# Scale guards on VectorE, and one product for two scales, in a fused attention and two-layer MoE kernel

## The chip, the cores and the metric

The kernel runs on one core of one Trainium2 chip. The metric is the device time of one execution in microseconds, the median of the runs; lower is better.

## The reference

An attention layer feeds two dense layers, over 12288 tokens of 128 channels:

```python
kv_flat = kv_pool.reshape(B, -1, C) @ w_sr        # 768 keys; k = v = kv_flat
s = scale * (q @ k.transpose(0, 2, 1))
a = np.exp(s - s.max(-1, keepdims=True))
x = (a / (a.sum(-1, keepdims=True) + 1e-09)) @ v
...
h = x @ w_in                                       # 128 -> 2048
x = (np.maximum(h, 0.0) + alpha * np.minimum(h, 0.0)) @ w_out
...
h = x @ w_in2
out = (h * (1.0 / (1.0 + np.exp(-1.702 * h)))) @ w_out2
```

## The kernel before, in words

The tokens are cut into 24 blocks of 512 (j = 0 to 23). Tokens lie along the free axis, channels along the 128 partitions. Every float32 operand is split into a float16 part (hi) and a float16 remainder (lo), and every product is three matmuls of 128x512 in PSUM (hi·hi, hi·lo, lo·hi). The TensorE steps of a block are:

- S j,t: the scores of 128 queries against 768 keys, four per block (six matmuls of 384 columns each)
- V j,k: the attention result X, six per block, one for each 128 keys
- L1 j,m and L2 j,m: the first dense layer by 16 slices m of the 2048 hidden channels; L2 sums into the result Y
- L3 j,m and L4 j,m: the second dense layer, likewise; L4 sums into the output

The steps of several blocks are mixed: while block 13's V and X are made, L1 and L2 of block 12 and L3 and L4 of blocks 10 and 11 run. A block's share is 210 matmuls of 512 columns and 24 of 384.

Around each L1 slice ScalarE takes relu from PSUM and VectorE the rest (prelu, L798); around each L3 slice ScalarE takes tanh (L837) and VectorE the rest of the gelu (L839). Then ScalarE rounds to float16 (hi, L774), and GpSimd, or for a few slices VectorE, subtracts for the remainder (lo, L777). L2 and L4 read these. In the text gelu 11,6 is the gelu of block 11's slice 6, and so on.

To split q, X and Y, each needs a power of two as its scale. Three times per block (Q, X and Y) this chain runs:

- a top: VectorE's absolute maximum of each partition (`td`, 128x1 in bfloat16, L613)
- a total: two matmuls of one column with a 128x128 matrix of ones (`total`, L623 for the tops and L624 for the constant `least`, which keeps the sum off zero). It takes one of the three PSUM banks (hb, hb, bk) that L1 and L3 use as well (`pool_h`)
- on VectorE, the exponent (`scp`, a bitwise and, L409), the scale (`scc`, L411), and for q also `qu`, for Y also `yu` (128x2)
- the hi part on ScalarE (L637) and the lo part on VectorE (L639)

For Y, ScalarE first copies the result to SBUF (`yc`, L818).

The order of instructions is fixed before the run. The first some 900 follow a list written out by hand (`ORDER`), and the rest a planner that places them by costs and due times. Each engine takes its instructions in that order, one by one, so an instruction that waits holds up all that follow it on its engine. q is loaded by the queue of SP, which also issues the transposes of the attention weights (`eh`, `el`) and the weights' loads.

Of the kernel before, what the change touches and what calls it, by code (L numbers as in the profile page):

```python
# [28 lines left out]
TB = 512  # L29
# [41 lines left out]
class Op:  # L71
# [41 lines left out]

# [271 lines left out]
def record(nc, T):  # L385
# [71 lines left out]
    def load(fn, size, w, prio, r=(), gate=None, name="load", eng="SP", late=1, occ=470):  # L457
        return op(eng, occ, int(size / 0.41e3), lambda: fn(S if eng == "SP" else A), r, w, prio, gate, name, dma=late)
# [7 lines left out]
    def load_wsr(e):  # L466
        e.dma_start(out=T["wsr"], in_=T["in_wsr"])
        A.preload_act_table(AF.Exp)
    load(load_wsr, 65536, [B["wsr"]], -999, eng="ACT", late=3700, occ=1900)
    load(lambda e: e.dma_start(out=T["al"], in_=T["in_al"]), 8192, [B["al"]], -997, r=[(B["wsr"], None, 7000)], eng="ACT", late=9000)  # L470
# [137 lines left out]

    qh, ql, qsc = {}, {}, {}

# [5 lines left out]

    def total(pool, cols_, least, prio):

        pm = pool.buf("pt")

        def f():
            for i, (c, _) in enumerate(cols_):
                mm(out=pm.ap[:, 0:1], lhsT=T["ones"], rhs=c(), start=i == 0, stop=False)  # L623
            mm(out=pm.ap[:, 0:1], lhsT=T["ones"], rhs=least, start=False, stop=True)  # L624
        op("PE", 28 + 28 * len(cols_), 0, f, [b for _, b in cols_] + [B["ones"]], [pm], prio, name="scmm")
        return pm

    def scale_of(d, pool, kc, kcb, prio):
        pm = total(pool, [(lambda: d.ap, d)], T["least"], prio)
        p, c = new("scp"), new("scc")  # L630
        small(lambda: ts(p.ap, pm.ap[:, 0:1].bitcast(I32), 0x7F800000, ALU.bitwise_and), [pm], [p], prio, occ=117)
        small(lambda: ts(c.ap, p.ap, -1.0, ALU.mult, kc(), ALU.add), [p] + kcb, [c], prio + .01, occ=110, dur=200)
        return c, p

    def parts(j, hi, lo, x, xb, c, prio, gate=None, psum=True):
# [4 lines left out]
                                                           op0=ALU.mult, op1=ALU.subtract), [xb, c, hi], [lo], prio + .01, gate, name="lo", lock=not psum)  # L640

    def q_prep(j, prio, gate=None, pool=None):
        t = q_t[j]
        pl.tag = f"Q{j}"
        d = top_of(j, lambda: cols(t.ap, j), t, False, prio, gate)
        c, p = scale_of(d, pool or pool_x, lambda: float(268 << 23), [], prio + .1)
        qh[j], ql[j] = new("qh"), new("ql")
        parts(j, qh[j], ql[j], lambda: cols(t.ap, j), t, c, prio + .2, gate, psum=False)
        qsc[j] = p
        if j:  # L650
            q_scale(j, prio + .3)
        pl.tag = ""

    def q_scale(j, prio):
        u, p = new("qu"), qsc[j]
        small(lambda: ts(u.ap, p.ap.bitcast(F32), T["kq"], ALU.mult), [p, B["kq"]], [u], prio, occ=125, dur=205)
        qsc[j] = u
# [81 lines left out]
    def x_prep(j, prio):  # L739
        x = xacc[j]  # L740
        pl.tag = f"X{j}"
        d = top_of(j, lambda: cols(x.ap, j), x, True, prio, None)
        c, p = scale_of(d, pool_h, lambda: T["kxc"], [B["kxc"]], prio + .1)
        xh[j], xl[j] = new("xh"), new("xl")
        parts(j, xh[j], xl[j], lambda: cols(x.ap, j), x, c, prio + .2)
        xsc[j] = p
        pl.tag = ""
# [64 lines left out]
    def y_prep(j):  # L812
# [6 lines left out]
        d = top_of(j, lambda: cols(y.ap, j), y, True, pr, None)  # L819
        c, p = scale_of(d, pool_h, lambda: T["kyc"], [B["kyc"]], pr + .5)  # L820
        u = new("yu")
        xp = xsc[j]
        small(lambda: ts(u.ap, T["kk"], p.ap.bitcast(F32), ALU.mult, xp.ap.bitcast(F32), ALU.mult), [B["kk"], p, xp], [u], pr + .6,
              occ=190, dur=280, lock=True)
# [81 lines left out]
    def rest():  # L906
# [3 lines left out]
        for j in range(NB):  # L910
            for m in range(KF):
                s = KF * j + m
                for jj in range(2, NB):
                    a = KF * jj - 25 + (ATT_AT[jj - 2] if jj < 4 else 0)
                    gate = lambda x: steps[s]
                    if s == max(a - 7, 0):
                        load_q(jj, s, steps.get(s - 1))
# [43 lines left out]

RINGS = {"q": 2, "fold": 2, "kv": 12, "raw": 6, "cv": 2, "td": 4, "scp": 16, "scc": 6, "qh": 2, "ql": 2, "qu": 4, "nm": 4,
         "sm": 4, "r": 4, "e": 2, "ah": 2, "alo": 2, "eh": 2, "el": 2, "xh": 2, "xl": 2, "yh": 3, "yl": 3, "yc": 1, "yu": 6,
# [4 lines left out]
def attn_moe_kernel(ctx: ExitStack, tc: tile.TileContext, q, kv, w_sr, w_in1, w_out1, alpha, w_in2, w_out2, out):  # L968
# [29 lines left out]
    for key in ("w1", "w2", "w3", "w4"):  # L998
        T["wm_" + key] = t("wm" + key, [NCW], BF16)
        T["wt_" + key] = t("wt" + key, [1], F32)  # L1000
        for x in ("we", "g", "u", "b"):
            T[x + "_" + key] = t(x + key, [1], I32)

    shapes = {"q": ([TB], F32), "raw": ([CW, 2], I32), "cv": ([CW], I32), "fold": ([KV2 // 2], F32), "td": ([1], BF16),
              "scp": ([1], I32), "scc": ([1], I32), "qh": ([TB], F16), "ql": ([TB], F16), "qu": ([1], F32), "nm": ([1], F32),
# [76 lines left out]
```

## Time and profile before

| | |
|---|---|
| time, median of 3 runs | 1244.88 us (1244.63 to 1245.29) |
| the profiled execution's own time | 1247.91 us |
| its span | 1246.1 us |
| TensorE busy | 1217.7 us, 98% |
| VectorE busy | 977.2 us, 78% |
| ScalarE busy | 1104.3 us, 89% |
| GpSimd busy | 799.1 us, 64% |
| mean granted TensorE clock | 0.998 |

The span is what the trace covers; the profiled execution's own time is 1.8 us longer, and it lies 3.0 us above the median of the runs without a profile. The busy shares are means over the start, where weights and keys are prepared, 18 blocks that repeat almost exactly, and a tail.

### The profile page before, as it was taken

What the parts mean: (1) busy time and instruction counts of PE and PEld (TensorE: products, weight loads), DVE (VectorE), ACT (ScalarE), POOL (GpSimd) and SP (SyncE); (2) the same over time, 40 slices, a digit from 0 to 9 for tenths busy, and PEclk for the clock granted to TensorE, in tenths of its full rate; (3) what the DMA queues carried; (4) which work ended last, traced back from release to release, by engine and by line L of the source; (5) the groups of instructions that cost most, each with busy time, mean ns of one, the idle gap of its engine ahead of it and who ended that gap; (6) DMA issues with size and microseconds to landing.
All of it is one profiled execution on the core that took longest, in us unless ns stands there. A gap on an engine that the chain in (4) does not pass through costs nothing.

```text
span 1246.1 us, 18536 instructions
## 1 busy us (share of the span) xinstructions
PE 1217.7 (98%) x5919; PEld 574.5 (46%) x5922; DVE 977.2 (78%) x1796; ACT 1104.3 (89%) x1939; POOL 799.1 (64%) x688
## 2 busy tenths in 40 slices
PE   6699999999999999999999999999999999999998
PEld 4444444444444444444444444444444444444443
DVE  5999997877777877777778777777787877776766
ACT  1799888989999999899999998999999989988988
POOL 1567556676667566666675666666766766666764
PEclk9999999999999999999999999999999999999999
DMA  9922222121222121212211222212121222120000
GB/s 378 219 51 46 40 56 47 35 55 26 56 49 33 43 47 35 55 31 51 55 27 43 47 42 49 40 41 56 27 49 41 47 43 48 34 47 14 9 9 18
DMA packets 165378, 66.69 MB, mean 54 GB/s; under 512 B 156448, under 2 KB 156576, under 8 KB 164256
## 3 DMA queue, kind: packets, MB, share of 16 engines
q1 hardware_dynamic: 164992, 65.43, 23.1%
q8 instruction: 46, 0.75, 0.3%
q14 instruction: 52, 0.43, 0.1%
q10 hardware_dynamic: 288, 0.07, 0.0%
HBM read 21.05 MB, written 6.29 MB: 22 GB/s over the span
## 4 chain that ended last, share of the span: by engine, by line
PE 64%; ACT 0%; issue 0%; DVE 0%; POOL 0%; POOLq 0%; ACTq 0%
PE bk L444 14%; PE bk L446 14%; PE bk L445 14%; PE hb L444 6%; PE hb L445 6%; PE hb L446 6%; PE sa L672 1%; PE sa L673 1%; PE sa L676 1%; POOL arena L777 0%; ACT arena L774 0%; ACT arena L837 0%; POOLq L1078 0%; ACT arena L796 0%; DVE arena L798 0%
## 5 line engine op out<-in xcount | busy, mean ns | idle before, releaser
L777 POOL TENSOR_TENSOR arena<-arena 128x512 f16<-128x512 f32 x656 | 763.0, 1182 | 401.9 <-ACT arena L774 205.1
L774 ACT CAST arena<-arena 128x512 f16<-128x512 f32 x740 | 443.6, 624 | 52.1 <-PE bk L445 19.4
L798 DVE SCALAR_TENSOR_TENSOR arena<-arena,oma,hb 128x512 f32<-128x512 f32 x280 | 207.7, 742 | 57.5 <-ACT arena L796 54.6
L839 DVE SCALAR_TENSOR_TENSOR arena<-arena,hb 128x512 f32<-128x512 f32 x225 | 153.7, 683 | 43.1 <-ACT arena L837 39.6
L796 ACT ACTIVATE arena<-hb 128x512 f32<-128x512 f32 x280 | 167.1, 597 | 8.7 <-POOL arena L777 4.7
L837 ACT ACTIVATE arena<-hb,yu 128x512 f32<-128x512 f32 x225 | 156.7, 696 | 13.0 <-PE hb L446 6.1
L446 PE MATMUL bk<-arena,w4h 128*128 128x512 f16 x384 | 145.5, 379 | 0.2 <-POOL arena L777 0.2
L446 PE MATMUL bk<-arena,w2h 128*128 128x512 f16 x384 | 145.5, 379 | 0.2 <-POOL arena L777 0.2
L444 PE MATMUL bk<-arena,w2h 128*128 128x512 f16 x384 | 145.5, 379 | 0.1
L445 PE MATMUL bk<-arena,w4l 128*128 128x512 f16 x384 | 145.5, 379 | 0.0
L445 PE MATMUL bk<-arena,w2l 128*128 128x512 f16 x384 | 145.5, 379 | 0.0
L444 PE MATMUL bk<-arena,w4h 128*128 128x512 f16 x384 | 145.5, 379 | 0.0
L711 DVE SCALAR_TENSOR_TENSOR alo<-sa,r,ah 128x768 f16<-128x768 f32 x88 | 89.4, 1016 | 53.7 <-ACT ah L696 52.4
L839 DVE SCALAR_TENSOR_TENSOR arena<-arena,bk 128x512 f32<-128x512 f32 x159 | 108.4, 682 | 23.3 <-ACT arena L837 23.1
L837 ACT ACTIVATE arena<-bk,yu 128x512 f32<-128x512 f32 x159 | 109.4, 688 | 17.6 <-PE bk L446 16.7
L444 PE MATMUL hb<-xh,w1h 128*128 128x512 f16 x280 | 106.3, 380 | 1.8 <-ACT xh L637 0.9
L446 PE MATMUL hb<-xl,w1h 128*128 128x512 f16 x280 | 106.3, 380 | 0.2 <-DVE xl L639 0.2
L445 PE MATMUL hb<-xh,w1l 128*128 128x512 f16 x280 | 106.3, 380 | 0.0
L682 DVE TENSOR_REDUCE nm<-sa 128x1 f32<-128x768 f32 x94 | 89.5, 952 | 12.4 <-PE hb L624 7.2
L777 DVE TENSOR_TENSOR arena<-arena 128x512 f16<-128x512 f32 x112 | 87.1, 778 | 6.3 <-ACT arena L774 4.7
L798 DVE SCALAR_TENSOR_TENSOR arena<-arena,oma,bk 128x512 f32<-128x512 f32 x104 | 77.3, 743 | 16.6 <-ACT arena L796 14.6
L689 ACT ACTIVATE sa<-sa,nm,qu 128x768 f32<-128x768 f32 x88 | 85.0, 966 | 1.2 <-DVE nm L409 1.1
(151 smaller groups left out, 2105.7 us busy)
## 6 DMA issues: line engine op xcount, KB each, us to landing
q<-in_q SPq DMA_DIRECT2D x24, 256.0 KB, 3.0
arena<-in_kv SPq DMA_DIRECT2D x12, 512.0 KB, 8.9
out<-arena SPq DMA_DIRECT2D x24, 256.0 KB, 2.0
raw<-in_moe_w_in SPq DMA_DIRECT2D x4, 1024.0 KB, 13.8
raw<-in_moe_w_out SPq DMA_DIRECT2D x4, 1024.0 KB, 12.1
eh<-ah SPq DMA_TRANSPOSE x96, 2.7
el<-alo SPq DMA_TRANSPOSE x96, 2.8
wsr<-in_w_sr ACTq DMA_DIRECT2D x1, 64.0 KB, 3.3
```

The costliest lines, as they stand in the source:

```text
L444: mm(out=o, lhsT=wh, rhs=xh, start=start, stop=False)
L445: mm(out=o, lhsT=wl, rhs=xh, start=False, stop=False)
L446: mm(out=o, lhsT=wh, rhs=xl, start=False, stop=stop)
L682: op("DVE", 868, 956, lambda: V.tensor_reduce(out=nm.ap, in_=s.ap[:, :, 0:HALF], axis=AX.XY, op=ALU.max, negate=True), [s], [nm], prio + . ...
L689: op("ACT", 890, 985, lambda: A.activation(dst(), src(), AF.Exp, bias=nm.ap, scale=qsc[j].ap, accum_out=sm.ap), [s, nm, qsc[j]], [e, sm], ...
L711: op("DVE", 933, 1019, lambda: V.scalar_tensor_tensor(out=al.ap, in0=dst(), scalar=r.ap, in1=ah.ap, op0=ALU.mult, op1=ALU.subtract), [e, r ...
L774: op("ACT", act(508, n), act(618, n), lambda: A.copy(cols(hi.ap, j), cols(g.ap, j)), [g], [hi], s + 1.2, name=f"{nm}h{j},{m}")
L777: lambda: (V if on else G).tensor_tensor(out=cols(lo.ap, j), in0=cols(g.ap, j), in1=cols(hi.ap, j), op=ALU.subtract),
L796: op("ACT", act(488, n), act(597, n), lambda: A.activation(cols(g.ap, j), cols(h.ap, j), AF.Relu, scale=-1.0), [h], [g], s + .3, name=f"re ...
L798: op("DVE", dve(658, n), dve(746, n), lambda: V.scalar_tensor_tensor(out=cols(g.ap, j), in0=cols(g.ap, j), scalar=T["oma"][:, m:m + 1], in ...
L837: op("ACT", act(581, n), act(687, n), lambda: A.activation(cols(g.ap, j), cols(h.ap, j), AF.Tanh, scale=u.ap[:, 0:1]), [h, u], [g], s + .3 ...
L839: op("DVE", dve(605, n), dve(687, n), lambda: V.scalar_tensor_tensor(out=cols(g.ap, j), in0=cols(g.ap, j), scalar=1.0, in1=cols(h.ap, j), ...
```

## The change

- The constant `least` and its matmul go from the totals of blocks 3 and up (`j > 2`), in Q, X and Y. In its place VectorE takes the maximum of the tops and 2^-60, in SBUF and in place, ahead of the total (called the guard here).
- In blocks 3 to 21, the top of the queries of block j + 2 is taken beside that of X of block j, into the two columns of a new tile `td2` (128x2, bfloat16). One guard of 128x2 and one matmul with two columns serve both, then one bitwise and of 128x2 (`scp2`), and the scales `scc` for X and `qcc` for the queries. The queries' own totals of blocks 5 to 23 go.
- From block 5 on a block's queries are loaded six steps m earlier.
- The planner's cost of a total goes from 28 + 28 ns for each of its matmuls to 62 ns for each, and that of loading `w_sr` changes; `ORDER` is renumbered and 19 entries shorter.

```diff
-    def total(pool, cols_, least, prio):
+    def total(pool, cols_, least, prio, n=1):
 
         pm = pool.buf("pt")
 
         def f():
             for i, (c, _) in enumerate(cols_):
-                mm(out=pm.ap[:, 0:1], lhsT=T["ones"], rhs=c(), start=i == 0, stop=False)
-            mm(out=pm.ap[:, 0:1], lhsT=T["ones"], rhs=least, start=False, stop=True)
-        op("PE", 28 + 28 * len(cols_), 0, f, [b for _, b in cols_] + [B["ones"]], [pm], prio, name="scmm")
+                mm(out=pm.ap[:, 0:n], lhsT=T["ones"], rhs=c(), start=i == 0, stop=least is None and i == len(cols_) - 1)
+            if least is not None:
+                mm(out=pm.ap[:, 0:n], lhsT=T["ones"], rhs=least, start=False, stop=True)
+        op("PE", 62 * len(cols_) + (62 if least is not None else 0), 0, f, [b for _, b in cols_] + [B["ones"]], [pm], prio, name="scmm")
         return pm
 
-    def scale_of(d, pool, kc, kcb, prio):
-        pm = total(pool, [(lambda: d.ap, d)], T["least"], prio)
+    def scale_of(d, pool, kc, kcb, prio, j=0):
+        if j > 2:
+            small(lambda: ts(d.ap, d.ap, 2.0 ** -60, ALU.max), [d], [d], prio)
+        pm = total(pool, [(lambda: d.ap, d)], None if j > 2 else T["least"], prio)
...
     def q_prep(j, prio, gate=None, pool=None):
         t = q_t[j]
         pl.tag = f"Q{j}"
-        d = top_of(j, lambda: cols(t.ap, j), t, False, prio, gate)
-        c, p = scale_of(d, pool or pool_x, lambda: float(268 << 23), [], prio + .1)
+        if j in qc:
+            c, p = qc[j]
+        else:
+            d = top_of(j, lambda: cols(t.ap, j), t, False, prio, gate)
+            c, p = scale_of(d, pool or pool_x, lambda: QC, [], prio + .1, j)
...
     def x_prep(j, prio):
         x = xacc[j]
         pl.tag = f"X{j}"
-        d = top_of(j, lambda: cols(x.ap, j), x, True, prio, None)
-        c, p = scale_of(d, pool_h, lambda: T["kxc"], [B["kxc"]], prio + .1)
+        if 2 < j < NB - 2:
+            t, d, p2, c, qc_ = q_t[j + 2], new("td2"), new("scp2"), new("scc"), new("qcc")
+            op("DVE", dve(593, TB), dve(692, TB), lambda: V.tensor_reduce(out=d.ap[:, 1:2], in_=t.ap, axis=AX.X, op=ALU.max, apply_absolute_value=True),
+               [t], [(d, 1)], prio, name="top")
+            op("DVE", dve(608, TB), dve(692, TB), lambda: V.tensor_reduce(out=d.ap[:, 0:1], in_=x.ap, axis=AX.X, op=ALU.max, apply_absolute_value=True),
+               [x], [(d, 0)], prio, name="top")
+            small(lambda: ts(d.ap, d.ap, 2.0 ** -60, ALU.max), [(d, 0), (d, 1)], [d], prio + .01)
+            pm = total(pool_h, [(lambda: d.ap, d)], None, prio + .1, 2)
+            small(lambda: ts(p2.ap, pm.ap[:, 0:2].bitcast(I32), 0x7F800000, ALU.bitwise_and), [pm], [p2], prio + .1, occ=117)
+            p, q = Half(p2, 0), Half(p2, 1)
+            small(lambda: ts(c.ap, p.ap, -1.0, ALU.mult, T["kxc"], ALU.add), [p2, B["kxc"]], [c], prio + .11, occ=110, dur=200)
+            small(lambda: ts(qc_.ap, q.ap, -1.0, ALU.mult, QC, ALU.add), [p2], [qc_], prio + .12)
+            qc[j + 2] = qc_, q
...
-                    if s == max(a - 7, 0):
+                    if s == max(a - (13 if jj > 4 else 7), 0):
                         load_q(jj, s, steps.get(s - 1))
```

What the change does to the order of instructions is seen at three places.

On VectorE, where block 13's X gets its scale. L613 (L765 after) is the top of X, L839 (L872) a gelu, L798 (L831) a prelu. Before:

```order
L839 SCALAR_TENSOR_TENSOR arena<-arena,bk_66 128x512
L613 TENSOR_REDUCE td_142<-bk_67 128x1
L798 SCALAR_TENSOR_TENSOR arena<-arena,oma,hb_580 128x512
L409 TENSOR_SCALAR scp_150<-bk_66 128x1
L411 TENSOR_SCALAR scc_163<-scp_150,kxc 128x1
L839 SCALAR_TENSOR_TENSOR arena<-arena,hb_579 128x512
```

And in the changed kernel:

```order
L872 SCALAR_TENSOR_TENSOR arena<-arena,hb_588 128x512
L765 TENSOR_REDUCE td_0_143<-bk_67 128x1
L831 SCALAR_TENSOR_TENSOR arena<-arena,oma,hb_587 128x512
L408 TENSOR_SCALAR td_0_143<-td_0_143 128x2
L408 TENSOR_SCALAR scp_2_147<-hb_588 128x2
L872 SCALAR_TENSOR_TENSOR arena<-arena,bk_66 128x512
L410 TENSOR_SCALAR scc_173<-scp_2_147,kxc 128x1
L410 TENSOR_SCALAR qcc_150<-scp_2_147 128x1
L408 TENSOR_SCALAR qu_181<-scp_2_147,kq 128x1
```

The guard stands behind the prelu, and the total on TensorE, which reads `td_0`, comes behind the guard; before, it could run as soon as the top was there. On TensorE this total has moved one step later, behind L2 12,10 instead of ahead of it.

On TensorE, where the queries of block 15 had their total: behind L2 12,15 (L444 to L446 with `w2`) and ahead of L3 11,7 (`w3h`). Before:

```order
L446 LDWEIGHTS w2h
L446 MATMUL bk_68<-arena,w2h 128x512
L623 LDWEIGHTS ones
L623 MATMUL hb_580<-td_139,ones 128x1
L624 LDWEIGHTS ones
L624 MATMUL hb_580<-least,ones 128x1
L444 LDWEIGHTS w3h
L444 MATMUL bk_66<-yh_201,w3h 128x512
```

And in the changed kernel, from the end of L2 12,15 on, with S 14,3 behind it:

```order
L445 LDWEIGHTS w2h
L445 MATMUL bk_68<-arena,w2h 128x512
L691 LDWEIGHTS qh_174
L691 MATMUL sa<-k_hi,qh_174 128x384
L692 LDWEIGHTS qh_174
```

The total is gone there, and L3 11,7 now stands ahead of L2 12,15. Y12's total comes after S 14,3, L1 13,3 and L4 11,3.

On VectorE near the start, where the queries of block 4 get their scale (L409, later L408, with `hb`), and gelu 0,7 (L839, later L872, with `hb` or `bk`) is near. Before:

```order
L777 TENSOR_TENSOR arena<-arena 128x512
L409 TENSOR_SCALAR scp_151<-hb_580 128x1
L711 SCALAR_TENSOR_TENSOR alo_190<-sa,r_182,ah_187 128x768
L777 TENSOR_TENSOR arena<-arena 128x512
L839 SCALAR_TENSOR_TENSOR arena<-arena,bk_66 128x512
L411 TENSOR_SCALAR scc_161<-scp_151 128x1
```

And in the changed kernel:

```order
L810 TENSOR_TENSOR arena<-arena 128x512
L408 TENSOR_SCALAR td_142<-td_142 128x1
L730 SCALAR_TENSOR_TENSOR alo_199<-sa,r_191,ah_196 128x768
L810 TENSOR_TENSOR arena<-arena 128x512
L872 SCALAR_TENSOR_TENSOR arena<-arena,hb_588 128x512
L408 TENSOR_SCALAR scp_160<-hb_587 128x1
```

The guard stands where the exponent stood, and the exponent behind gelu 0,7. On TensorE the total of block 4's queries moved from ahead of L3 0,7 to two steps behind it, and L3 0,4 then takes the bank of L3 0,7 and not of that total.

## Rows read from the trace of the kernel before

**Rows 1.** The page, part 1: busy time, share of the span, instructions.

```profile
PE 1217.7 (98%) x5919; PEld 574.5 (46%) x5922; DVE 977.2 (78%) x1796; ACT 1104.3 (89%) x1939; POOL 799.1 (64%) x688
```

**Rows 2.** Timeline, TensorE: first matmuls of L1 5,0 and L1 22,0 (start, duration).

```profile
271.24 0.38 PE L444 MATMUL bk<-xh,w1h 128*128 128x512 f16 x1
...
1113.09 0.38 PE L444 MATMUL bk<-xh,w1h 128*128 128x512 f16 x1
```

**Rows 3.** Timeline, TensorE: X13's total, L2 12,10, and L1 12,14's first matmul.

```profile
660.70 0.17 PE L623 MATMUL bk<-td,ones 128*128 128x1 bf16 x1
...
660.75 0.38 PE L444 MATMUL bk<-arena,w2h 128*128 128x512 f16 x1
...
661.39 0.38 PE L444 MATMUL hb<-xh,w1h 128*128 128x512 f16 x1
```

**Rows 4.** Timeline around Q15's total: L2 12,15's end, the total, L3 11,7; gelu 11,6.

```profile
674.11 0.68 DVE L839 SCALAR_TENSOR_TENSOR arena<-arena,bk 128x512 f32<-128x512 f32 x1
...
674.46 0.38 PE L446 MATMUL bk<-arena,w2h 128*128 128x512 f16 x1
...
674.70 0.16 PE L624 MATMUL hb<-least,ones 128*128 128x1 bf16 x1
...
674.85 0.38 PE L444 MATMUL bk<-yh,w3h 128*128 128x512 f16 x1
```

**Rows 5.** Timeline, VectorE and GpSimd behind X13's top (in brackets: idle before, releaser).

```profile
660.21 0.74 DVE L798 SCALAR_TENSOR_TENSOR arena<-arena,oma,hb 128x512 f32<-128x512 f32 x1
...
660.78 1.15 POOL L777 TENSOR_TENSOR arena<-arena 128x512 f16<-128x512 f32 x1 [0.71 <-ACT arena L774]
...
660.94 0.16 DVE L409 TENSOR_SCALAR scp<-bk 128x1 int32<-128x1 int32 x1
...
661.13 0.21 DVE L411 TENSOR_SCALAR scc<-scp,kxc 128x1 int32<-128x1 int32 x1
```

**Rows 6.** Tile yu: its 24 instructions (min/median/max ns, first and last start); timeline of one.

```profile
L411 DVE TENSOR_SCALAR yu<-kk,scp,scp x24: 272/278/1269, 98.1 to 1209.5; 128x2 f32<-128x2 f32 x24
...
183.77 1.27 DVE L411 TENSOR_SCALAR yu<-kk,scp,scp 128x2 f32<-128x2 f32 x1
...
183.85 1.17 POOL L777 TENSOR_TENSOR arena<-arena 128x512 f16<-128x512 f32 x1 [1.93 <-DVE scc L411]
```

**Rows 7.** Timeline: Y12's copy, top and total.

```profile
675.41 0.59 ACT L818 COPY yc<-bk 128x512 f32<-128x512 f32 x1
...
676.03 0.69 DVE L613 TENSOR_REDUCE td<-bk 128x1 bf16<-128x512 f32 x1 [0.51 <-ACT yc L818]
...
677.12 0.17 PE L623 MATMUL hb<-td,ones 128*128 128x1 bf16 x1
```

**Rows 8.** Timeline, the start: T2,1's maximum and Q3's total; L3 0,4 and gelu 0,7.

```profile
88.35 0.94 DVE L682 TENSOR_REDUCE nm<-sa 128x1 f32<-128x768 f32 x1
...
88.77 0.17 PE L623 MATMUL bk<-td,ones 128*128 128x1 bf16 x1
...
120.27 0.38 PE L444 MATMUL hb<-yh,w3h 128*128 128x512 f16 x1
...
121.76 0.69 DVE L839 SCALAR_TENSOR_TENSOR arena<-arena,bk 128x512 f32<-128x512 f32 x1
```

**Rows 9.** Waits of TensorE (us in total, times, longest).

```profile
PE bk L444 <- DVE arena L798: 0.8, 1, 0.8
```

**Rows 10.** Timeline: a VectorE cast among GpSimd's instructions; GpSimd around Q15's total.

```profile
228.70 3.57 POOL L777 TENSOR_TENSOR arena<-arena 128x512 f16<-128x512 f32 x3
...
230.47 0.79 DVE L771 CAST arena<-arena 128x512 f16<-128x512 f32 x1
...
671.94 5.62 POOL L777 TENSOR_TENSOR arena<-arena 128x512 f16<-128x512 f32 x5 [0.65 <-POOL arena L777]
```

**Rows 11.** The page, part 6: the queries' loads (KB each, us from issue to landing).

```profile
q<-in_q SPq DMA_DIRECT2D x24, 256.0 KB, 3.0
```

More of the change, by code (lines that the diff above doesn't have):

```diff
@@ L468, in load_wsr @@
         A.preload_act_table(AF.Exp)
-    load(load_wsr, 65536, [B["wsr"]], -999, eng="ACT", late=3700, occ=1900)
+    load(load_wsr, 266500, [B["wsr"]], -999, eng="ACT", occ=1900)
     load(lambda e: e.dma_start(out=T["al"], in_=T["in_al"]), 8192, [B["al"]], -997, r=[(B["wsr"], None, 7000)], eng="ACT", late=9000)
@@ L606, in conv @@
         pl.tag = ""
-    qh, ql, qsc = {}, {}, {}
+    qh, ql, qsc, qc = {}, {}, {}, {}
     def top_of(j, x, xb, psum, prio, gate):
@@ L640, in parts, with __init__, ap, whole @@
                                                            op0=ALU.mult, op1=ALU.subtract), [xb, c, hi], [lo], prio + .01, gate, name="lo", lock=not psum)
+    class Half:
+        def __init__(self, b, k):
+            self.b, self.k = b, k
+        @property
+        def ap(self):
+            return self.b.ap[:, self.k:self.k + 1]
+    def whole(b):
+        return b.b if isinstance(b, Half) else b
+    QC = float(268 << 23)
     def q_prep(j, prio, gate=None, pool=None):
@@ L655, in q_scale @@
         u, p = new("qu"), qsc[j]
-        small(lambda: ts(u.ap, p.ap.bitcast(F32), T["kq"], ALU.mult), [p, B["kq"]], [u], prio, occ=125, dur=205)
+        small(lambda: ts(u.ap, p.ap.bitcast(F32), T["kq"], ALU.mult), [whole(p), B["kq"]], [u], prio, occ=125, dur=205)
         qsc[j] = u
@@ L741, in x_prep @@
         pl.tag = f"X{j}"
-        d = top_of(j, lambda: cols(x.ap, j), x, True, prio, None)
-        c, p = scale_of(d, pool_h, lambda: T["kxc"], [B["kxc"]], prio + .1)
+        if 2 < j < NB - 2:
[11 more added lines that the diff above has]
+            qc[j + 2] = qc_, q
+        else:
+            d = top_of(j, lambda: cols(x.ap, j), x, True, prio, None)
+            c, p = scale_of(d, pool_h, lambda: T["kxc"], [B["kxc"]], prio + .1, j)
         xh[j], xl[j] = new("xh"), new("xl")
@@ L819, in y_prep @@
         d = top_of(j, lambda: cols(y.ap, j), y, True, pr, None)
-        c, p = scale_of(d, pool_h, lambda: T["kyc"], [B["kyc"]], pr + .5)
+        c, p = scale_of(d, pool_h, lambda: T["kyc"], [B["kyc"]], pr + .5, j)
         u = new("yu")
         xp = xsc[j]
-        small(lambda: ts(u.ap, T["kk"], p.ap.bitcast(F32), ALU.mult, xp.ap.bitcast(F32), ALU.mult), [B["kk"], p, xp], [u], pr + .6,
+        small(lambda: ts(u.ap, T["kk"], p.ap.bitcast(F32), ALU.mult, xp.ap.bitcast(F32), ALU.mult), [B["kk"], p, whole(xp)], [u], pr + .6,
               occ=190, dur=280, lock=True)
@@ L959, in record @@
     return pl
-RINGS = {"q": 2, "fold": 2, "kv": 12, "raw": 6, "cv": 2, "td": 4, "scp": 16, "scc": 6, "qh": 2, "ql": 2, "qu": 4, "nm": 4,
+RINGS = {"q": 2, "fold": 2, "kv": 12, "raw": 6, "cv": 2, "td": 4, "td2": 2, "scp2": 4, "qcc": 3, "scp": 16, "scc": 6, "qh": 2, "ql": 2, "qu": 4, "nm": 4,
          "sm": 4, "r": 4, "e": 2, "ah": 2, "alo": 2, "eh": 2, "el": 2, "xh": 2, "xl": 2, "yh": 3, "yl": 3, "yc": 1, "yu": 6,
@@ L1002, in attn_moe_kernel @@
             T[x + "_" + key] = t(x + key, [1], I32)
-    shapes = {"q": ([TB], F32), "raw": ([CW, 2], I32), "cv": ([CW], I32), "fold": ([KV2 // 2], F32), "td": ([1], BF16),
+    shapes = {"q": ([TB], F32), "raw": ([CW, 2], I32), "cv": ([CW], I32), "fold": ([KV2 // 2], F32), "td": ([1], BF16), "td2": ([2], BF16), "scp2": ([2], I32), "qcc": ([1], I32),
               "scp": ([1], I32), "scc": ([1], I32), "qh": ([TB], F16), "ql": ([TB], F16), "qu": ([1], F32), "nm": ([1], F32),
```

27 rows, old and new, of the table ORDER are left out of this document.

## The prediction

> **What bounds the kernel now.** The page's busy shares come first: TensorE is busy for 98% of the span [rows 1], and no other engine comes near that. The table of its waits comes next: it names next to none outside the start and a few waits of under 1 us [rows 9]. The timeline then shows how regular the middle is: from L1 5,0 to L1 22,0 there are 17 blocks in (1113.09 - 271.24) = 841.85 us, 49.52 us each [rows 2]. So the time is what TensorE is given to do, and each microsecond in which it waits is a microsecond of the result. An edit gains only what it takes off TensorE, and it loses whatever TensorE has to wait for. I therefore read every place where the change puts VectorE between two TensorE steps, and asked whether VectorE is in time.
>
> **What is removed.** Counted in the diff, 82 one-column matmuls go: 19 totals of queries with two each (38), `least` in the totals of Q3 and Q4 (2), and of X and Y in blocks 3 to 23 (42). Their records last 0.16 us, but that is latency. What they cost on TensorE is read from start to start: X13's total begins at 660.70 and the next product at 660.75 [rows 3], so two matmuls cost 0.05 us and one 0.025. All lie on TensorE's path: 82 x 0.025 = 2.05 us off.
>
> [...]
>
> A wait goes too. Behind Q15's total, L3 11,7 begins at 674.85, 0.15 us after the total's second matmul at 674.70, not 0.025 [rows 4]. Gelu 11,6 ends at 674.11 + 0.68 = 674.79, and 0.06 later L3 starts: the total had taken a bank, so L3 waited for that gelu's. Without the total L3 finds another bank, and without the queries' top at that place VectorE is earlier. The block's pattern repeats for Q6 to Q23, so 18 x 0.12 = 2.2 us off. The bounds are 0 and 2.2, for the bank could come late from elsewhere. I take all of it.
>
> **What is added at X, 19 times.** The top of block j + 2's queries goes in where VectorE has gaps, and the guard is small, but its place matters. VectorE's order puts it behind prelu 12,13, which starts at 660.21 and lets the next instruction start at 660.94 [rows 5]. If nothing is in the way it lasts like the 128x1 exponent that stood there, 0.16 us, and ends at 661.10. With 0.06 from VectorE to TensorE (as in rows 4), the total could run at 661.16. In the new order the total stands behind L2 12,10, where TensorE arrives at 661.39 - 0.05 = 661.34 [rows 3]. Then it costs nothing.
>
> But GpSimd is in the way. Its subtraction starts at 660.78 and runs to 661.93 [rows 5], so it is already running when the guard comes. It was released by ScalarE's rounding, which waits for a ring buffer that TensorE's L4 10,13 frees one step after V 13,5; V 13,5 also releases the top. So both move with TensorE, and I expect the 0.16 us between the two to stand in each block. What does a two-element VectorE instruction do under a running GpSimd one? The 128x1 instructions do nothing special: `scc` takes its 0.21 us at 661.13 under that same subtraction [rows 5]. The only TENSOR_SCALAR of two elements from SBUF to SBUF in this kernel is `yu`, 24 times: 0.278 us at the median, but 1.27 at most [rows 6]. In that longest one it starts at 183.77, a GpSimd subtraction starts 0.08 later and ends at 185.02, and `yu` ends at 185.04. It waited for GpSimd to the end.
>
> The guard differs from `yu` in that it is bfloat16 and has one source besides a constant. The bounds for its wait are therefore 0 (as `scc`) and the whole rest of the subtraction (as `yu`). It is nearest to `yu` in shape, source and destination, so I take the upper one: it ends at 661.93 + 0.02 = 661.95, the total starts at 662.01, and TensorE stands for 662.01 - 661.34 = 0.67 us. Nothing covers that, since TensorE takes its steps in order. Queued behind the guard on VectorE are the exponent, gelu 11,2 and the two scales; they are late by about as much as TensorE, so I add nothing for them. I count 18 blocks (the first of the 19, X3, lies in a stretch that is not regular): 18 x 0.66 = 11.9 us on.
>
> [...]
>
> **What is added at Y.** Now Y's top is followed by gelu 11,7, then the guard, and the total must wait for it. The guard is 128x1, so GpSimd costs it nothing. When is the total due? It ran at 677.12 [rows 7]. Q15's total with its wait goes (0.18) and L4 11,3 (0.65, as L2 12,10 in rows 3) moves ahead of it, so TensorE arrives at 677.59. When is the guard done? L2 12,15 now runs behind L3 11,7, one step later: its last matmul starts at 674.46 + 0.65 [rows 4] and ends at 675.49. Copy 0.59, top and gelu about 0.6 each (0.69 and 0.68, overlapped by some 0.08 when they follow directly), guard 0.16 and 0.06 each way between engines give 677.6. So there is no margin, and whatever ScalarE is late with the copy is paid. Before, it was late by 675.41 - 674.84 = 0.57 us. Ahead of the copy, Q15's hi and a tanh now come in and a rounding goes out, while TensorE gives the relu and tanh of L1 13,1 and L3 11,6 one step sooner. I take 0.1 us, with bounds of 0 and 0.5: 18 x 0.1 = 1.8 us on.
>
> **What is added at the start.** The list fixes two bad places. Q3's guard stands where the exponent stood, behind T2,1's maximum, which runs from 88.35 to 89.29; the total ran at 88.77 [rows 8]. It must now wait until 89.40: 0.6 us on. Around block 4, L3 0,4 takes the bank of L3 0,7 and waits for gelu 0,7, which ends at 122.45 [rows 8]; by the order it would start at 120.27 + 0.65 = 120.92, behind L2 1,10. So it starts at 122.50: 1.6 us on. Later waits may swallow some, so the bounds for both together are 0.8 and 2.5.
>
> **What moves.** With the totals of Q5 and later gone, the irregular stretch near 180 us loses some of its waits. I take off 0.8, the longest [rows 9]; the bounds are 0 and 1.7. The queries' loads go to SP earlier, from behind the transposes of one tile to between two of them, and their tops come earlier too. A load lands in 3.0 us [rows 11]. By the order and VectorE's gaps there I estimate that the top needs it about 4 us after its issue, so I cost the move at nothing; if one lands 1 us later than that, the prelus queued behind the top, and L1 behind them, are late by up to as much.
>
> **Sum.** -2.05 - 2.2 + 11.9 + 1.8 + 0.6 + 1.6 - 0.8 = +10.85 us on the profiled execution's own time of 1247.91 us, 1258.8. That execution lies 3.0 us above the median of the runs, so 1255.7 there.
>
> **Rivals.**
> - *The guard is not held up* (the rival on the other side). [...] Then 11.9 goes from the sum: -1.1, or 1243.8 us. It speaks for it that no row shows a bfloat16 instruction of two elements; against it, that `yu` has the same shape. It decides at a wait of 1.1 / 18 = 0.06 us per block: below that the change is no loss. With Y's chain at 0 and the start at 0.8 it reaches 1240.5, with Y's at 0.3 it is 1247.4.
> - *Y's chain is late*. ScalarE stays 0.5 us late with the copy: 18 x 0.4 = 7.2 more, 1262.9 beside the held-up guard, 1251.0 without it. For it speaks that ScalarE has hardly a gap there; against it, the earlier relu and tanh.
> - *Q15's lo is held up*. It moves to about 674, where GpSimd has five subtractions in a row from 671.94 to 677.56 [rows 10]. If it must wait for one or two of them, gelu 11,6, prelu 13,2 and Y's top behind it are late by up to 0.9 us: 16 more, 1272. Against it: a cast at 230.47 in the middle of three such subtractions took 0.79 us [rows 10], so VectorE gets its turn between two of them.
>
> **How the numbers follow.** Held-up guard 0.68, not held up 0.22, Y's chain or Q15's lo late 0.08, anything else 0.02. The time is that of the first, 1255.7; its own range is 1252 to 1259. The guard that isn't held up ends at 1240.5 to 1247.5, so the range has to reach into it: 1242.5 to 1259.5 leaves out about 1 in 10 on each side. A difference of 0.2%, 2.5 us, is about what a measurement of this kernel can tell from no change. Of the 0.22, 0.1 lies below 1242.4, 0.1 between and 0.02 above; the first and third case are slower but for 0.03. With the rest: faster 0.12, same 0.14, slower 0.74.
>
> **What would show it.** Right: a guard of 128x2 of about 1.0 us in each block from 4 to 21, that ends with GpSimd's subtraction, and the total of X 0.06 behind it with an idle TensorE of about 0.67 ahead; a period near 50.0 us. Wrong: a guard of 0.15 to 0.28 us and a period near 49.4. L3 11,7 should follow directly on its neighbour; at Y the total should stand for at most 0.1 to 0.2; Q3's total should start near 89.4 and L3 0,4 near 122.5. I would be most wrong if the guard goes through untouched, or if VectorE's later place lets GpSimd end first.

## The result, and the profile after

The changed kernel takes 1258.3 us (1255.8 to 1260.0, six runs) against 1246.4 for the kernel before (1244.6 to 1248.9, six runs): a ratio of 1.0093, 95% interval 1.0075 to 1.0111. It is 11.6 us slower by the ratio, 11.9 by the medians. The forecast was 10.85 us slower. By the two profiled executions' own times the difference is 1258.36 - 1247.91 = 10.45 us.

The page of the changed kernel begins with the busy times and shares, as [rows 1] did.

```profile
PE 1219.9 (97%) x5839; PEld 570.7 (45%) x5839; DVE 1004.5 (80%) x1821; ACT 1098.9 (87%) x1939; POOL 805.6 (64%) x688
```

TensorE has 80 records fewer (82 fewer of the totals, two more of others) and is busy no less. (This line alone shows little: a product's record lasts 0.38 us and the next starts 0.22 us behind it, so up to 0.16 us of a wait lies under a record. Of the 0.67 us below the profile lists 0.51.) Its waits show more: us in total, times, and the longest.

```profile
PE hb L622 <- DVE td L408: 8.6, 17, 0.5
PE bk L445 <- POOL arena L810: 1.1, 3, 0.6
PE bk L622 <- DVE td L408: 1.0, 3, 0.5
```

L622 is the total and L408 the guard. The first row wasn't there before: 17 totals wait for a two-column guard. One of them in the timeline, block 13's X (start, duration; in brackets the idle time before and its releaser), to be read against [rows 3] and [rows 5]:

```profile
665.48 0.74 DVE L831 SCALAR_TENSOR_TENSOR arena<-arena,oma,hb 128x512 f32<-128x512 f32 x1
...
665.85 1.16 POOL L810 TENSOR_TENSOR arena<-arena 128x512 f16<-128x512 f32 x1 [0.31 <-ACT arena L807]
...
666.14 0.90 DVE L408 TENSOR_SCALAR td<-td 128x2 bf16<-128x2 bf16 x1
666.20 0.38 PE L445 MATMUL bk<-arena,w2h 128*128 128x512 f16 x1
...
667.09 0.16 PE L622 MATMUL hb<-td,ones 128*128 128x2 bf16 x1 [0.51 <-DVE td L408]
```

The guard comes 0.29 us after GpSimd's subtraction has begun and ends at 667.04, 0.03 behind it. The total follows 0.05 later. L2 12,10's last matmul started at 666.20, so TensorE would have been ready for the total 0.22 us later, at 666.42: it stood for 0.67 us. VectorE's instructions of that kind, grouped by shape (busy time, mean ns of one):

```profile
L408 DVE TENSOR_SCALAR td<-td 128x2 bf16<-128x2 bf16 x19 | 19.6, 1030 | 0.0
...
L408 DVE TENSOR_SCALAR td<-td 128x1 bf16<-128x1 bf16 x25 | 3.7, 148 | 0.0
```

All 19 two-column guards take 1.03 us on the mean, the 25 one-column guards 0.148. The guard takes as long as what is left of the subtraction that was running when it started: each of the 19 ends 0.03 us behind that subtraction, the shortest after 0.32 us (block 4), the longest after 1.10. In 14 of blocks 6 to 21 the guard starts only 0.08 us behind the subtraction, as in block 12:

```profile
615.66 1.16 POOL L810 TENSOR_TENSOR arena<-arena 128x512 f16<-128x512 f32 x1 [0.71 <-ACT arena L807]
615.74 1.10 DVE L408 TENSOR_SCALAR td<-td 128x2 bf16<-128x2 bf16 x1
```

At Y (block 12), to be read against [rows 7]:

```profile
680.85 0.38 PE L445 MATMUL bk<-arena,w2h 128*128 128x512 f16 x1
...
681.46 0.65 ACT L851 COPY yc<-bk 128x512 f32<-128x512 f32 x1
...
682.14 0.69 DVE L612 TENSOR_REDUCE td<-bk 128x1 bf16<-128x512 f32 x1 [0.19 <-ACT yc L851]
...
682.75 0.68 DVE L872 SCALAR_TENSOR_TENSOR arena<-arena,hb 128x512 f32<-128x512 f32 x1
...
683.12 0.38 PE L445 MATMUL bk<-arena,w4h 128*128 128x512 f16 x1
...
683.34 0.15 DVE L408 TENSOR_SCALAR td<-td 128x1 bf16<-128x1 bf16 x1
...
683.54 0.16 PE L622 MATMUL bk<-td,ones 128*128 128x1 bf16 x1
683.57 0.38 PE L443 MATMUL hb<-yh,w3h 128*128 128x512 f16 x1
```

L2 12,15 (its last matmul is the first row) ends at 681.23, and the copy starts 0.23 us later. Then come top, gelu 11,7, guard and total: the guard ends at 683.49, and the total starts at 683.54 where TensorE was ready at 683.12 + 0.22 = 683.34. It stands for 0.20 us. L3 11,8 follows at once.

Near the start, to be read against [rows 8]:

```profile
87.50 0.38 PE L445 MATMUL hb<-xl,w1h 128*128 128x512 f16 x1
88.35 0.16 PE L622 MATMUL bk<-td,ones 128*128 128x1 bf16 x1 [0.47 <-DVE td L408]
...
119.88 0.38 PE L444 MATMUL bk<-arena,w2l 128*128 128x512 f16 x1
120.83 0.38 PE L445 MATMUL bk<-arena,w2h 128*128 128x512 f16 x1 [0.57 <-POOL arena L810]
121.97 0.38 PE L443 MATMUL hb<-yh,w3h 128*128 128x512 f16 x1 [0.77 <-DVE arena L872]
```

Q3's total stands for 88.35 - 87.72 = 0.63 us. L2 1,10's third matmul waits 0.73 for GpSimd's remainder, and L3 0,4 behind it 0.92 for gelu 0,7.

Two rows give the period, as [rows 2] did: the first matmuls of L1 5,0 and L1 22,0.

```profile
271.86 0.38 PE L443 MATMUL hb<-xh,w1h 128*128 128x512 f16 x1
...
1124.21 0.38 PE L443 MATMUL hb<-xh,w1h 128*128 128x512 f16 x1
```

(1124.21 - 271.86) / 17 = 50.14 us, against 49.52 before.

### The profile page after: what moved, and what is told of

Its sections match the earlier page's. It is cut to its first block, busy times and chain, and to the rows that moved or that the text cites. A ratio compares the mean times of both kernels' runs of the same rounds, so it can differ in the third digit from the quotient of the medians.

```text
span 1256.6 us, 18326 instructions
## 1 busy us (share of the span) xinstructions
PE 1219.9 (97%) x5839; PEld 570.7 (45%) x5839; DVE 1004.5 (80%) x1821; ACT 1098.9 (87%) x1939; POOL 805.6 (64%) x688
## 5 line engine op out<-in xcount | busy, mean ns | idle before, releaser
L872 DVE SCALAR_TENSOR_TENSOR arena<-arena,hb 128x512 f32<-128x512 f32 x261 | 178.5, 684 | 56.7 <-ACT arena L870 54.2
L831 DVE SCALAR_TENSOR_TENSOR arena<-arena,oma,hb 128x512 f32<-128x512 f32 x262 | 194.2, 742 | 31.0 <-ACT arena L829 27.4
L870 ACT ACTIVATE arena<-hb,yu 128x512 f32<-128x512 f32 x261 | 183.0, 702 | 12.3 <-PE hb L445 10.9
L829 ACT ACTIVATE arena<-hb 128x512 f32<-128x512 f32 x262 | 160.1, 612 | 23.0 <-PE hb L445 18.3
L444 PE MATMUL bk<-arena,w4l 128*128 128x512 f16 x384 | 145.5, 379 | 0.0
L444 PE MATMUL bk<-arena,w2l 128*128 128x512 f16 x384 | 145.5, 379 | 0.0
L872 DVE SCALAR_TENSOR_TENSOR arena<-arena,bk 128x512 f32<-128x512 f32 x123 | 83.9, 682 | 37.6 <-ACT arena L870 37.4
L831 DVE SCALAR_TENSOR_TENSOR arena<-arena,oma,bk 128x512 f32<-128x512 f32 x122 | 90.6, 743 | 13.4 <-ACT arena L829 10.8
L444 PE MATMUL hb<-xh,w1l 128*128 128x512 f16 x262 | 99.6, 380 | 0.0
L443 PE MATMUL hb<-yh,w3h 128*128 128x512 f16 x261 | 98.8, 379 | 0.8 <-DVE arena L872 0.8
L445 PE MATMUL hb<-yl,w3h 128*128 128x512 f16 x261 | 98.9, 379 | 0.0
L444 PE MATMUL hb<-yh,w3l 128*128 128x512 f16 x261 | 98.8, 379 | 0.0
L870 ACT ACTIVATE arena<-bk,yu 128x512 f32<-128x512 f32 x123 | 85.3, 693 | 12.2 <-PE bk L445 10.6
```

What stands on the lines that cost most here:

```text
L443: mm(out=o, lhsT=wh, rhs=xh, start=start, stop=False)
L444: mm(out=o, lhsT=wl, rhs=xh, start=False, stop=False)
L445: mm(out=o, lhsT=wh, rhs=xl, start=False, stop=stop)
L829: op("ACT", act(488, n), act(597, n), lambda: A.activation(cols(g.ap, j), cols(h.ap, j), AF.Relu, scale=-1.0), [h], [g], s + .3, name=f"re ...
L831: op("DVE", dve(658, n), dve(746, n), lambda: V.scalar_tensor_tensor(out=cols(g.ap, j), in0=cols(g.ap, j), scalar=T["oma"][:, m:m + 1], in ...
L870: op("ACT", act(581, n), act(687, n), lambda: A.activation(cols(g.ap, j), cols(h.ap, j), AF.Tanh, scale=u.ap[:, 0:1]), [h, u], [g], s + .3 ...
```

## The experiments

The theory at this point: GpSimd holds the two-column guard up, and that is X's 0.67 us. By it that wait goes where two guards of one column stand in its place, or where the guard runs clear of a subtraction. The rivals: the guard's place in VectorE's queue makes it late anyway; a bfloat16 instruction of two elements is slow by itself; or the shared product or the moved loads are at fault. In the first four runs the order of every engine is that of the changed kernel; only the instructions named are exchanged. Where no order is mentioned, the same holds for later ones.

**Two guards of one column.**

```diff
-            small(lambda: ts(d.ap, d.ap, 2.0 ** -60, ALU.max), [(d, 0), (d, 1)], [d], prio + .01)
+            small(lambda: (ts(d.ap[:, 1:2], d.ap[:, 1:2], 2.0 ** -60, ALU.max), ts(d.ap[:, 0:1], d.ap[:, 0:1], 2.0 ** -60, ALU.max))[1], [(d, 0), (d, 1)], [d], prio + .01)
```

> The 128x2 guard of X is issued as two guards of 128x1, one per column, at the same place of VectorE's order; the order of every engine stays that of the changed kernel. [...] Rival, the place behind the prelu and VectorE's queue make the total late: TensorE still stands 0.6 us there and the time stays at 1257 to 1258.

Measured: 1246.1 us, ratio 0.9994 to the kernel before (0.9985 to 1.0004). That is 12.2 us less than the changed kernel. In its timeline, at block 12's X:

```profile
610.30 1.16 POOL L810 TENSOR_TENSOR arena<-arena 128x512 f16<-128x512 f32 x1 [0.71 <-ACT arena L807]
...
610.39 0.21 DVE L408 TENSOR_SCALAR td<-td 128x1 bf16<-128x1 bf16 x2
...
610.65 0.38 PE L445 MATMUL bk<-arena,w2h 128*128 128x512 f16 x1
610.87 0.17 PE L622 MATMUL hb<-td,ones 128*128 128x2 bf16 x1
```

Both halves run within 0.21 us under the same GpSimd subtraction, and the total stands right behind L2 11,10. The place is the same, the data are the same, and only the shape differs: the queue isn't the cause. In this profile one block's X (13) still stood for 0.4 us, though its two halves took 0.21 us as well (they came late, at 660.63); the others of blocks 5 to 21 didn't.

**The same guard, 0.7 us earlier.**

```diff
-            op("DVE", ..., lambda: V.tensor_reduce(out=d.ap[:, 0:1], in_=x.ap, ...),
+            op("DVE", ..., lambda: (V.tensor_reduce(out=d.ap[:, 0:1], in_=x.ap, ...), ts(d.ap, d.ap, 2.0 ** -60, ALU.max))[1],
...
-            small(lambda: ts(d.ap, d.ap, 2.0 ** -60, ALU.max), [(d, 0), (d, 1)], [d], prio + .01)
+            small(lambda: None, [(d, 0), (d, 1)], [d], prio + .01)
```

> The same 128x2 guard, issued directly behind X's top and ahead of the prelu; all else as in the changed kernel. [...] Rival, a 128x2 bfloat16 instruction in place is slow by itself: it still takes 1.0 us, the total starts at about the time of TensorE's arrival or up to 0.2 us behind it, and prelu and gelu behind are 0.9 us late: 1248 to 1252.

Measured: 1245.9 us, ratio 0.9997 (0.9986 to 1.0008). GpSimd and VectorE at block 13's X, and the group of these guards:

```profile
655.97 2.27 POOL L810 TENSOR_TENSOR arena<-arena 128x512 f16<-128x512 f32 x2 [2.78 <-ACT arena L807]
...
658.30 0.17 DVE L408 TENSOR_SCALAR td<-td 128x2 bf16<-128x2 bf16 x1
...
658.60 1.16 POOL L810 TENSOR_TENSOR arena<-arena 128x512 f16<-128x512 f32 x1 [0.36 <-ACT arena L807]
...
L408 DVE TENSOR_SCALAR td<-td 128x2 bf16<-128x2 bf16 x19 | 4.3, 228 | 0.7
```

GpSimd's pair of subtractions ends at 658.24, the guard starts at 658.30 and takes 0.17. So do all 17 from block 5 on, clear of a subtraction. The mean of 0.23 has two more in it, which still came while one was running: block 3's took 0.53 us and block 4's 0.89 (the next row), and both ended 0.03 us behind it.

```profile
211.69 0.89 DVE L408 TENSOR_SCALAR td<-td 128x2 bf16<-128x2 bf16 x1
```

So the instruction isn't slow by itself. Both runs together show the cause: two columns, and a GpSimd instruction that is running.

**Products again in place of all guards, the shared product kept.**

```diff
-            small(lambda: ts(d.ap, d.ap, 2.0 ** -60, ALU.max), [d], [d], prio)
+            small(lambda: None, [d], [d], prio)
...
-            if least is not None:
-                mm(out=pm.ap[:, 0:n], lhsT=T["ones"], rhs=least, start=False, stop=True)
+            mm(out=pm.ap[:, 0:n], lhsT=T["ones"], rhs=T["least"][:, 0:n] if least is None else least, start=False, stop=True)
```

X's guard likewise issues nothing, and the constant gets a second column.

> No guard anywhere: each total gets its second one-column (for X two-column) product with the constant again, 44 more matmuls than the changed kernel; the queries' shared product and the order of all else stay. Theory (the guards on VectorE cost the time, sharing gains it): X's waits (about 12 us), Y's waits of 0.2 us in 17 blocks (3.5 us) and Q3's 0.6 us go, 44 x 0.025 = 1.1 us comes back: 1258.3 - 15 = 1243, some 3 us under the kernel before. Rival, the moved loads or the shared product are at fault: it stays over 1250.

Measured: 1244.2 us, ratio 0.9982 (0.9971 to 0.9993); 1.2 us over what was expected. Sharing the product and moving the loads cost nothing that this run shows; the guards did. A wait at Y is left, one step further on, 17 times 0.09 us (start of the total's two matmuls and of L3 11,8):

```profile
677.22 0.17 PE L622 MATMUL bk<-td,ones 128*128 128x1 bf16 x1
677.25 0.16 PE L623 MATMUL bk<-least,ones 128*128 128x1 bf16 x1
677.36 0.38 PE L443 MATMUL hb<-yh,w3h 128*128 128x512 f16 x1
```

L3 11,8 starts 0.11 us behind the second matmul and not 0.025. It takes the bank that gelu 11,7 has to free.

**All guards directly behind their tops.**

```diff
         op("DVE", ..., lambda: (V.tensor_reduce(out=d.ap, in_=x(), ...), j > 2 and ts(d.ap, d.ap, 2.0 ** -60, ALU.max))[0], [xb], [d], prio, gate, name="top")
```

> Every guard directly behind its top: X's of 128x2 as in the run before this one, and those of 128x1 for Y, Q3, Q4, X22 and X23. Theory: Y's total waited 0.2 us because the guard stood behind a gelu; now it is done 0.6 us before TensorE comes, so 17 x 0.2 = 3.5 us and Q3's 0.6 us go beside X's 12: about 1242. Rival, Y's wait is ScalarE's late copy: 0.1 to 0.2 us stays at Y, and the time is within 1 us of the run with X's guard early.

Measured: 1249.3 us, ratio 1.0018 (1.0007 to 1.0029): a miss, on the side of neither theory. It is 3.3 us slower than the run with only X's guard early. At block 12's Y:

```profile
676.45 0.69 DVE L612 TENSOR_REDUCE td<-bk 128x1 bf16<-128x512 f32 x1 [0.20 <-ACT yc L851]
677.18 0.16 DVE L408 TENSOR_SCALAR td<-td 128x1 bf16<-128x1 bf16 x1
677.25 0.68 DVE L872 SCALAR_TENSOR_TENSOR arena<-arena,hb 128x512 f32<-128x512 f32 x1
...
677.43 0.38 PE L445 MATMUL bk<-arena,w4h 128*128 128x512 f16 x1
677.65 0.17 PE L622 MATMUL bk<-td,ones 128*128 128x1 bf16 x1
677.98 0.38 PE L443 MATMUL hb<-yh,w3h 128*128 128x512 f16 x1 [0.16 <-DVE arena L872]
```

The total no longer waits (677.65 = 677.43 + 0.22). But L3 11,8 now waits 0.3 us for gelu 11,7: with the guard ahead of it, that gelu starts 0.80 us behind the top's start and not 0.61. In the two traces this makes 17 x 0.3 in place of 17 x 0.2, 1.7 us of the 3.3. In these two executions another 1.6 lie ahead of 70.3 us, where both kernels run the same instructions, so by the traces the early guard costs 1.7. At Y two things are due at one time, the total's guard and the gelu whose bank the next step takes. Putting one first makes the other late.

**One step between Y's total and L3 j,8.** After the planning, two neighbours on TensorE are exchanged, on top of the run before:

```diff
+        pe = [o for o in done if o.eng == "PE"]
+        for a, b in zip(pe, pe[1:]):
+            if a.name.startswith("L3 ") and a.name.endswith(",8") and b.name.startswith("L2 ") and b.name.endswith(",0"):
+                a.start, b.start = b.start, a.start
```

> The run with every guard directly behind its top was 3.3 us slower than the one with X's alone there: TensorE now waits 0.3 us for gelu j,7, one step behind Y's total, where L3 j,8 takes that gelu's bank. Here L3 j,8 and the step behind it, L2 j+2,0, are exchanged on TensorE; nothing else is changed. Theory (the gelu's bank is the limit at Y, and the guard ahead of the gelu only made it later): the step of 0.65 us put between covers the wait, 17 x 0.3 = 5 us go, 1249.3 - 5 = 1244. Rival (the wait comes from the chain of Y's scale, or L2 j+2,0 in its turn waits for Y's top and copy): it stays at 1247 to 1249.

Measured: 1254.1 us, ratio 1.0068 (1.0055 to 1.0080), a second miss, also on the side of neither theory. The wait at L3 11,8 is gone, and a longer one has come at L3 11,10. TensorE, then ScalarE and VectorE ahead of it:

```profile
684.49 0.38 PE L449 MATMUL bk<-arena,w4h 128*128 128x512 f16 x1
685.19 0.38 PE L447 MATMUL hb<-yh,w3h 128*128 128x512 f16 x1 [0.32 <-DVE arena L835]
...
681.08 0.69 ACT L874 ACTIVATE arena<-hb,yu 128x512 f32<-128x512 f32 x1 [0.60 <-PE hb L449]
...
683.77 0.59 ACT L833 ACTIVATE arena<-hb 128x512 f32<-128x512 f32 x1
...
684.39 0.75 DVE L835 SCALAR_TENSOR_TENSOR arena<-arena,oma,hb 128x512 f32<-128x512 f32 x1 [0.26 <-ACT arena L833]
```

ScalarE stands for 0.6 us ahead of tanh 11,8 (L874 at 681.08; 0.25 in the run before), because L3 11,8 now comes a step later. Behind it in ScalarE's order are Y's hi, an exp and relu 13,4 (683.77); prelu 13,4 waits for that relu, and L3 11,10 for that prelu's bank, 685.19 - 684.71 = 0.48 us in each block. I had asked whether the moved step would find its bank, and not who waits for its result.

**The mixed version, with the same exchange.** X's guard of two columns early, products everywhere else.

> X's guard of 128x2 directly behind its top; all other guards are products with the constant again (25 more matmuls than the changed kernel, 0.65 us); L3 j,8 and L2 j+2,0 exchanged as in the run before this one. Theory: neither X's nor Y's total waits, and L3 j,8 finds its bank: against the run with X's guard early alone 17 x 0.2 = 3.5 us less at Y, 0.2 less at the start, 0.65 more: 1243. Rival, a wait moves on to a later step: 1245 to 1246.

Measured: 1254.6 us, ratio 1.0076 (1.0063 to 1.0090). The same wait at L3 j,10, and the same miss.

**The same, with block 4's total at its old place.** In `ORDER`, Q4's total goes back ahead of L3 0,7, its exponent to where the guard stood, and L3 0,4 ahead of L2 1,10.

> As the run before this one, and near 120 us the total of block 4's queries, its exponent, and L3 0,4 ahead of L2 1,10 stand again as in the kernel before. Theory: the 0.73 us that L2 1,10 waited for GpSimd's remainder and the 0.93 us that L3 0,4 waited for gelu 0,7 go: 1.6 us less than the run before this one, about 1241, some 5 us under the kernel before. Rival, VectorE or GpSimd is late at the next step there: less than 0.8 us is gained.

Measured: 1253.1 us, ratio 1.0060 (1.0048 to 1.0072), 1.5 us less than the run before it. The level is a miss for the reason given. The two ratios overlap, so the times alone don't show the difference; the traces do: with the old order the two waits near 120 us, 0.93 and 0.69 us in the run before, are gone, and from L1 0,8 to L1 2,8 TensorE takes 1.4 us less. The expected 1.6 is nearly that.

**The guard marked for turns with GpSimd.**

```diff
-            small(lambda: ts(d.ap, d.ap, 2.0 ** -60, ALU.max), [(d, 0), (d, 1)], [d], prio + .01)
+            small(lambda: ts(d.ap, d.ap, 2.0 ** -60, ALU.max), [(d, 0), (d, 1)], [d], prio + .01, lock=True)
```

> The changed kernel with one word more: X's guard is marked in the planner as an instruction that takes turns with GpSimd, as yu is. From block 4 on the planner then gives nearly the same order, with the guard behind the prelu as before. Theory: the mark doesn't move the guard out of the subtraction, so X's wait of 0.67 us per block stays: 1257 to 1259. Rival, an order that is different in blocks 3 and 4 sets another pattern and the wait goes: below 1250.

Measured: 1258.4 us, ratio 1.0111 (1.0094 to 1.0129): as the changed kernel. The planner then counts the wait, and from block 5 on it puts the guard behind the prelu all the same, though other instructions change places; X's totals still stand for 0.67 us in each block.

**Products, block 4's total at its old place, no exchange.**

> The run with products in place of all guards, and near 120 us the total of block 4's queries, its exponent, and L3 0,4 ahead of L2 1,10 as in the kernel before; L3 j,8 stays where the changed kernel has it. Theory: the two waits near 120 us, 1.6 us, go, as they did in the pair of runs with the exchanged step (1.5): 1244.2 - 1.5 = 1242.7, 0.2 to 0.3% under the kernel before. Rival: the start's gain is swallowed by a later wait, 1244.

Measured: 1243.0 us, ratio 0.9982 (0.9970 to 0.9994). The time is near the 1242.7 expected, but the ratio is that of the run with products and block 4 as changed, so the times alone don't show the gain of 1.5 us. The traces do: from L1 0,8 to L1 2,8 TensorE takes 68.3 us against 69.7 there, and the two waits near 120 us are gone.

**X's guard early, products elsewhere, block 4 as before, no exchange.**

> As the run before this one, but X's floor is the 128x2 guard directly behind X's top in place of a second product. Theory: 19 products less, 0.5 us, and the guard lies clear of GpSimd's subtractions: 1242.2. Rival: VectorE's extra 0.2 to 0.3 us behind X's top makes prelu and gelu late, and TensorE waits elsewhere: 1243 to 1246.

Measured: 1244.1 us, ratio 0.9985 (0.9975 to 0.9996). It can't be told from the run before; whether the 19 products less gain anything stays open. Its trace has three longer waits that the run before doesn't have: 0.47 us in block 4, where the guard still came while GpSimd ran, and 0.74 and 0.44 near 360 us. So the rival came true in part.

**Gelu j-1,7 ahead of Y's top.** On top of the run before:

```diff
+        dve = [o for o in done if o.eng == "DVE"]
+        for a, b in zip(dve, dve[1:]):
+            if a.name == "top" and a.keys[0][0] == "Y" and b.name.startswith("gelu") and b.name.endswith(",7"):
+                a.start, b.start = b.start, a.start
```

> As the run before this one, and on VectorE the gelu j-1,7 and Y j's top are exchanged, the gelu first. Without a guard Y's total needs only the top, and L3 j-1,8 behind it needs that gelu's bank; the gelu's tanh ends before Y's copy does. Theory: the top still ends as TensorE comes to Y's total, and the 0.09 us that L3 j-1,8 waits go: 17 x 0.09 = 1.5 us less than the run before this one, about 1241. Rival: the top is now late, and Y's total waits 0.1 to 0.3 us: 1242 to 1246.

Measured: 1241.7 us, ratio 0.9962 (0.9948 to 0.9976): faster than the kernel before by 4.7 us going by the ratio and 3.6 by the medians, and 2.4 less than the run before it. At block 12's Y:

```profile
670.32 0.68 DVE L851 SCALAR_TENSOR_TENSOR arena<-arena,hb 128x512 f32<-128x512 f32 x1
670.92 0.69 DVE L591 TENSOR_REDUCE td<-bk 128x1 bf16<-128x512 f32 x1
...
671.80 0.17 PE L601 MATMUL bk<-td,ones 128*128 128x1 bf16 x1
671.83 0.16 PE L603 MATMUL bk<-least,ones 128*128 128x1 bf16 x1
671.85 0.38 PE L422 MATMUL hb<-yh,w3h 128*128 128x512 f16 x1
```

The top ends at 671.61, in time for the total at 671.80, and L3 11,8 starts 0.02 behind the second matmul. Both waits are gone. The 17 waits of L3 j,8 were worth 1.4 us; the rest of the 2.4 is about what the two single waits near 360 us took, which this trace doesn't have either.

## Why the prediction was right, point by point

**What bounds the kernel.** Right. TensorE's waits are in the time, and what took them away gave it back: X's 17 waits of 0.67 us are 11.4, and the run of two halves took 12.2 less than the changed kernel.

**The matmuls removed, and the wait of L3 j,7.** The first term, 2.05 us, wasn't measured by itself; 82 records did go, and behind a total the next product still starts 0.03 later (683.54 and 683.57). The second held: around the place of the old total of the queries no wait of TensorE is left in the middle of the trace: L3 11,7 starts at 679.77, 0.21 us behind the product before it at 679.56. The last run agrees: with the waits gone, a kernel with 57 of the 82 removals is 0.4% faster than before.

**X's guard.** Right in place, mechanism and size: 0.67 us predicted and measured, in blocks 6 to 21; block 5's was 0.62, block 3's 0.45 (at 170.83), and block 4 had none. 17 times 0.67 is 11.4 us where 18 times 0.66 were put down. That `yu` was the row to go by, and not `scc`, is shown by the halves and by the early guard. One detail was off: the guard came 0.08 us behind GpSimd's start in 14 of these blocks and 0.29 in block 13, not 0.16. It changes nothing, since all 19 guards ended 0.03 us behind the subtraction wherever they started.

In the runs a guard of 128x2 took 1.03 us on the mean when a subtraction was running as it came, and 0.17 clear of one. Two instructions of 128x1 went through under one in 0.21 us together. Why two columns wait and one doesn't, no run shows.

**Y's guard.** The mechanism held: there is no margin, and ScalarE's lateness with the copy, which starts 0.23 us behind L2 12,15's end, is paid. But the term was too small: 0.20 us in a block, not 0.1, so 17 x 0.2 = 3.4 us and 0.4 in block 3 where 1.8 were put down; it lay within the bounds of 0 and 0.5. What the prediction didn't see is the second wait beneath it: L3 j-1,8 needs the bank of the gelu that stands between top and guard. That is why the early guard made it worse.

**The start.** Right: 0.63 us at Q3 (0.6 predicted) and 0.73 + 0.92 = 1.65 near 120 us (1.6 predicted). The second is made up in another way than I wrote. Part of it, 0.73, is L2 1,10, which came a step earlier and waited for GpSimd; the wait for gelu 0,7 took only the rest. Both end at the same point, set by the gelu: it ends at 121.92, and L3 0,4 starts at 121.97.

**What moves.** The queries' loads and tops cost nothing that the runs show. For the stretch near 180 us 0.8 was taken off. Before, its three waits came to 1.68 us (0.23, 0.78 and 0.67 between 181 and 188 us). They are gone, and X3's wait of 0.45 has come, so the gain is nearer to 1.2 us, not tested by itself.

**The sum.** 10.85 predicted, 10.45 by the profiled executions, 11.6 by the ratio. In the trace the terms with their measured sizes (the first two as predicted) come to -2.05 - 2.2 + 11.4 + 3.8 + 0.6 + 1.65 - 1.2 = 12.0. Two things that no term foresaw take off 1.65. The changed kernel's TensorE is ready for Q3's total 88.77 - 87.72 = 1.05 us earlier (its waits for an exp at the very start are 5.0 us against 6.4). That start differs between executions: the first matmul of L1 0,8 came between 68.6 and 71.7 us in the first four runs, which execute the same instructions up to there as the changed kernel. And from L1 22,0 to the end it takes 132.4 us against 133.0, 0.6 less beyond the matmuls removed there; several waits of 0.14 to 0.27 us are gone, which no run tests. So the sum was nearer than its terms: X 0.5 less, Y 2.0 more, the stretch near 180 us 0.4 less, the start 1.05 and the end 0.6 less nearly cancel. X's term was sized rightly; that the whole came out within 0.4 us is luck.

**The rivals.** "The guard is not held up" fell to the trace. Its forecast of 1243.8 can be set beside the run of two halves, which is what the change would be without that wait: 1246.1, 2.3 us more, of which Y's 2.0 are most. "Q15's lo is held up" didn't come: it took 0.78 us at 679.50 within GpSimd's row of subtractions. By the trace it was GpSimd that gave way: the subtraction that started at 679.69, 0.19 us behind the lo, took 1.61 us, and three together 3.84, while five took 5.62 before [rows 10].

## What to carry to other kernels

Count an added instruction of a second engine not by its duration but by what is running beside it and what waits behind it: a guard of 256 numbers cost 0.67 us of TensorE in each block, and the matmul that it replaced 0.025. Where an instruction may have to take turns with GpSimd, find the row of the same shape, and look at what GpSimd does at that moment of the block. And when a wait is taken away, ask what is due next and who waits for the step that is moved: two of the cures here made the time worse, by 3.3 us (1.7 by the traces) and by 4.8.

## What was not expected of the hardware

A VectorE instruction on two columns of 2 bytes took six times as long as in the clear (1.03 us on the mean against 0.17) because a GpSimd instruction was running when it started: it ended 0.03 us behind that one, however much of it was left (all 19 times, after 0.32 to 1.10 us). Two instructions on one column each went through under the same GpSimd instruction in 0.21 us together. It is cheaper here to issue two.
